# Two layer-norm tiles by ScalarE root, both sines later, first weights from ScalarE's queue, and a new order of loads and work

## The chip, the cores and the metric

The kernel runs on one core of a Trainium2 chip. The metric is the device time of one execution in microseconds. A core has TensorE (PE, matrix products into PSUM), VectorE (DVE), ScalarE (ACT, activations from tables that are loaded one set at a time), GpSimd (POOL), and SyncE (SP, which here only issues DMAs). ScalarE can issue DMAs too; its queue and SyncE's are separate queues on the same 16 DMA engines.

## The reference

```python
def _layernorm(x, axis=-1, eps=1e-5):
    m = jnp.mean(x, axis=axis, keepdims=True); v = jnp.var(x, axis=axis, keepdims=True)
    return (x - m) / jnp.sqrt(v + eps)

xn = _layernorm(A_q)                                   # 2048 x 512, bf16
# s: long convolution along the 2048 positions, one filter per channel
k_shift = sum over t of 4 taps: k shifted by t, times shift_k
kv = k_shift * A_v
y  = irfft(rfft(pad(kv)) * rfft(pad(ssm_k)))[:2048] + kv * ssm_D
s  = xn * y
# g: gated feed-forward, 512 -> 1792 -> 512
h  = gelu_tanh(xn @ w_gate) * (xn @ w_up)
g  = silu(h @ w_down)
out = A_q + s * g
```

## The kernel before

There are two halves on one core. The **feed-forward half** works on 16 tiles of 128 positions in four quarters q of four tiles. For each quarter: `ln` (statistics on VectorE, variance plus epsilon, the power -0.5 on GpSimd, then the normalised tile `XN`), a transpose of `XN` into `xnT`, 14 `unit`s m (a gate product with `Wg` and an up product with `Wu` of four matmuls each, GELU of the gate on ScalarE into `GE`, product on VectorE into `HT`), then `down`. In quarter 0 the transposes are done by TensorE against `ident`, and the units 0 and 1 are cut into pieces, so that they can begin with the first tiles: their products are single tiles of 128 columns (line 646, 128x128), and gelu and product are halves of 256 columns (lines 1197 and 1199). In quarters 1 to 3 the transpose is one DMA on SP (line 902), which needs the four normalised tiles of its quarter.

The **convolution half** turns the filter `Hn` (four blocks `h0` to `h3`, four `STREAM_TRANSPOSE`s on VectorE, line 931) and the shifted keys times values (lines 1017 to 1025, VectorE) into spectra by matmuls against tables of sines: `F1`/`FT` (first stage, lines 969 and 958) and `TF`, `MI` (second stage, line 1040). The tables are computed in the kernel: integer phases on VectorE (`f_mul`, `f_phase`, `m_parts`, `m_product`, `m_phase`), sines on ScalarE (`f_sin` writes `F1`, `m_sin` writes `TAB`), products `m_prod` twice and a sum `m_sum` on VectorE (lines 752 and 755) give `TF`, and `m_turn` (line 767, ScalarE, four instructions) gives `TFA` and `TFB`, which two DMA transposes on SP turn into `MI`.

**The order.** Each piece of work is a task, numbered in the order in which the code adds it. `SEQ` is a list of task numbers written out by hand; a number with `b` takes the task's second engine. Each engine runs its own tasks in the order in which they stand in `SEQ`, and waits in that order: an instruction whose input is not there holds up all behind it on its engine. Which PSUM bank or buffer slot a task gets is decided at build time from planned durations (`LAND` holds the planned landing times of loads). `ORDER` is the order of loads, all issued by SP.

In the kernel before, the orders around the start are:

- SP: x00 x01 x02 (tiles 0, 1, and 2 with 3 of quarter 0), wg0 wu0 (weights of units 0 and 1, 256 KB each), wg1 wu1, D, h0 h1 h2 h3, wg2 wu2, x1, taps, k0, ... v0 v1 k3 v2 v3, then the transpose of quarter 1.
- ACT: sine table load, `f_sin`, variance of tile 0, `m_sin` with the load of the GELU table, variance of tile 2, copies of the transposed tiles, gelus of units 0 and 1 and the copy of tile 3, gelu 2, gelu 4, last half of gelu 0, gelu 5, `swap_rows`, `m_turn`, gelu 6, ...
- DVE: phases, statistics and normalised tiles 0 to 3 with the two `m_prod`s and `m_sum` among them, halves of the products of units 0 and 1, h0 and h1 transposed, product 2, h2 transposed, product 4, h3 transposed, product 5, last half of product 0, product 6, statistics of tiles 4 to 7, ...
- PE: 12 warm-up matmuls, transposes of tiles 0 and 1, pieces of units 0 and 1 with the transposes of tiles 2 and 3, units 2, 4, 5, 3, 6, 9, 7 in part, and then the first filter stage (line 969).
- POOL: constants, four powers (tiles 0 to 3), four tap copies (line 998), the power of quarter 1, the addition `h_fold` (line 938), the powers of quarters 3 and 2.

Of the kernel before, what the change touches and what calls it, by code (L numbers as in the profile page):

```python
# [417 lines left out]
def build_kernel(nc, A_q, A_k, A_v, A_shift_k, A_ssm_k, A_ssm_D, B_w_gate, B_w_up, B_w_down, out):  # L418
    with ExitStack() as es0:
# [334 lines left out]
        def m_sum():
            D(lambda h: h.tensor_tensor(TF[:], TM[0][:], TM[1][:], ALU.add), R_TM, [R_MF])

        def sin(T, V, R_V, R_T, n=128):
            trk.op("ACT", lambda h: h.activation(T, V, ACTF.Sin, bias=COLS[0:n, 0:1], scale=SIN_SCALE), r=[*R_V, R_cols], w=[R_T])

        def m_sin(e):  # L760
            sin(TAB[:], PH[:], [R_PH], R_TAB)
            trk.op("ACT", lambda h: h.activation(COLS[:, 1:2], COLS[:, 0:1], ACTF.Gelu_apprx_tanh), r=[R_cols], w=[R_col1])
# [10 lines left out]
        def f_sin(e):  # L773
            sin(F1, C32[:].rearrange("p a c -> p (a c)"), [R_C32], R_F1)
        S.add([("ACT", 510.0)], f_sin, r=[bFP, bcq, bwarm], w=[bF1])
        S.add([("DVE", 800.0), ("ACT", 1600.0)], swap_rows, r=[bF1], w=[bFS])
# [87 lines left out]
        def ln(q):  # L864
# [4 lines left out]
            for h in range(1 if q else 4):  # L869
# [5 lines left out]
                def var(e, hd, ts=ts):  # L875
                    if e == "ACT":
                        return hd.activation(mv[:, ts, 2:3], mv[:, ts, 1:2], ACTF.Identity, bias=EPSC[:, 0, :], scale=1.0)
                    return hd.tensor_scalar(mv[:, ts, 2:3], mv[:, ts, 1:2], LN_EPS, None, ALU.add)  # L878
# [498 lines left out]
```

## Time and profile before

| | |
|---|---|
| median of 3 runs | 187.17 us (186.51 to 187.7) |
| span of the profiled execution | 185.7 us |
| own time of the profiled execution | not given beside its span; the median lies 1.5 us above the span |
| PE busy | 178.5 us (96%) |
| DVE busy | 165.4 us (89%) |
| ACT busy | 141.4 us (76%) |
| POOL busy | 11.9 us (6%) |
| bytes moved by DMA | 48.38 MB |

A row of the timeline gives start and duration in us, engine, line, operation, output<-input with shapes, and in brackets the idle time of the engine before it and what ended that. Rows that are merged have a count (x4), and their duration runs from the first start to the last end. Matmuls overlap one another, so that four of them of 512 columns show 1.03 us but follow each other every 0.87 us; instructions of VectorE overlap by some 0.08 us too.

### The profile page before, as it was taken

What the parts mean: (1) busy time and instruction counts of PE and PEld (TensorE: products, weight loads), DVE (VectorE), ACT (ScalarE), POOL (GpSimd) and SP (SyncE); (2) the same over time, 40 slices, a digit from 0 to 9 for tenths busy, and PEclk for the clock granted to TensorE, in tenths of its full rate; (3) what the DMA queues carried; (4) which work ended last, traced back from release to release, by engine and by line L of the source; (5) the groups of instructions that cost most, each with busy time, mean ns of one, the idle gap of its engine ahead of it and who ended that gap; (6) DMA issues with size and microseconds to landing.
All of it is one profiled execution on the core that took longest, in us unless ns stands there. A gap on an engine that the chain in (4) does not pass through costs nothing.

```text
span 185.7 us, 3808 instructions
## 1 busy us (share of the span) xinstructions
PE 178.5 (96%) x1513; PEld 77.9 (42%) x1522; DVE 165.4 (89%) x247; ACT 141.4 (76%) x205; POOL 11.9 (6%) x26
## 2 busy tenths in 40 slices
PE   8799799999999999999999999999999999999992
PEld 3564344444443443434443433433334344445451
DVE  6989999999999999999267998998999997694795
ACT  3745989956689999987965798898988686326971
POOL 4500044100000000020200000000000000000000
PEclk9999999999999999999999999999999999999999
DMA  5999999999964578979979998589746233699355
GB/s 132 337 406 376 280 346 369 397 416 257 257 232 165 186 243 266 325 241 369 222 271 205 335 333 276 177 272 317 254 163 217 76 116 119 205 359 389 141 180 196
DMA packets 38683, 48.38 MB, mean 260 GB/s; under 512 B 9483, under 2 KB 28427, under 8 KB 38666
## 3 DMA queue, kind: packets, MB, share of 16 engines
q1 hardware_dynamic: 32138, 39.76, 65.6%
q10 hardware_dynamic: 6528, 8.39, 13.8%
q8 instruction: 12, 0.20, 0.5%
q14 instruction: 5, 0.04, 0.1%
HBM read 27.39 MB, written 14.68 MB: 227 GB/s over the span
## 4 chain that ended last, share of the span: by engine, by line
PE 77%; DVE 9%; DMA 5%; ACT 5%; issue 2%; SPq 0%; ACTq 0%
PE psall L646 63%; PE psall L1040 5%; DMA Hn<-in_A_ssm_k_dram 4%; PE psall L1236 3%; PE psall L958 2%; PE psall L969 2%; DMA X<-in_A_q_dram 1%; ACT GE L1206 1%; DVE KTM L1021 1%; PE psall L1290 1%; ACT FT L637 1%; DVE HTr L931 1%; DVE G L1307 1%; DVE G L1258 1%; DVE G L1319 1%
## 5 line engine op out<-in xcount | busy, mean ns | idle before, releaser
L646 PE MATMUL psall<-xnT,Wu 128*128 128x512 bf16 (+1 forms) x248 | 55.9, 359 | 0.0
L646 PE MATMUL psall<-xnT,Wg 128*128 128x512 bf16 (+1 forms) x248 | 55.6, 359 | 0.0
L1206 ACT ACTIVATE GE<-psall 128x512 bf16<-128x512 f32 x54 | 32.2, 621 | 11.1 <-PE psall L646 7.0
L646 PE MATMUL psall<-Wd,HT 128*128 128x512 bf16 (+1 forms) x173 | 38.1, 367 | 0.7 <-ACT GE L1206 0.2
L646 PEld LDWEIGHTS psall<-xnT,Wu 128*128 128x128 bf16 x248 | 22.0, 98 | 26.5 <-issue 3.2
L646 PEld LDWEIGHTS psall<-xnT,Wg 128*128 128x128 bf16 x248 | 21.9, 98 | 26.1 <-issue 2.0
L1215 DVE TENSOR_TENSOR HT<-psall,GE 128x512 bf16<-128x512 f32 x36 | 24.2, 682 | 3.8 <-PE psall L646 3.6
L637 ACT ACTIVATE BO<-psall 128x1024 bf16<-128x1024 f32 x21 | 21.1, 1024 | 6.2 <-PE psall L1290 4.7
L646 PEld LDWEIGHTS psall<-Wd,HT 128*128 128x128 bf16 x182 | 16.3, 98 | 20.7 <-issue 3.4
L1143 DVE TENSOR_TENSOR HSW<-KB,HSW 128x2048 bf16<-128x2048 bf16 x16 | 19.2, 1215 | 0.0
L637 ACT ACTIVATE KB<-psall 128x1024 bf16<-128x1024 f32 x15 | 15.2, 1030 | 3.6 <-PE psall L1040 3.6
L637 ACT ACTIVATE HSW<-psall 128x1024 bf16<-128x1024 f32 x15 | 15.0, 1036 | 1.6 <-PE psall L1040 1.6
L1023 DVE TENSOR_TENSOR KAC<-KAC,KTM 128x2048 bf16<-128x2048 bf16 x12 | 14.6, 1214 | 0.0
L1021 DVE TENSOR_TENSOR KTM<-KK,SKB 128x2048 bf16<-128x2048 bf16 x12 | 14.6, 1213 | 0.0
L637 ACT ACTIVATE XN<-psall 128x1024 bf16<-128x1024 f32 x10 | 10.3, 1028 | 4.6 <-PE psall L969 3.3
L1236 PE MATMUL psall<-Wd,HT 128*64 128x512 bf16 (+1 forms) x112 | 12.5, 366 | 0.0
L1247 ACT ACTIVATE G<-psall 128x512 bf16<-128x512 f32 x12 | 6.9, 596 | 7.0 <-PE psall L646 7.0
L637 ACT ACTIVATE U__73<-psall 128x512 bf16<-128x512 f32 x18 | 11.5, 654 | 0.1
L867 DVE BATCH_NORM_STATS2 stats<-X 128x6 f32<-128x512 bf16 x16 | 10.5, 676 | 0.5 <-DMA X<-in_A_q_dram 0.5
L880 POOL TENSOR_TENSOR mv<-mv,NHALF 128x1 f32<-128x1 f32 (+1 forms) x7 | 6.5, 926 | 62.3 <-DVE mv L878 60.0
L1143 DVE TENSOR_TENSOR KB<-KB,HSW 128x2048 bf16<-128x2048 bf16 x8 | 9.6, 1216 | 0.0
L1166 DVE TENSOR_TENSOR HSW<-HSW 128x2048 bf16<-128x2048 bf16 x8 | 9.6, 1216 | 0.0
(89 smaller groups left out, 177.5 us busy)
## 6 DMA issues: line engine op xcount, KB each, us to landing
BH<-ZH SPq DMA_DIRECT2D x8, 512.0 KB, 4.6
HSW<-HSW SPq DMA_DIRECT2D x16, 256.0 KB, 3.6
BK<-ZK SPq DMA_DIRECT2D x8, 512.0 KB, 5.3
ZI<-BO ACTq DMA_DIRECT2D x16, 256.0 KB, 2.2
BI<-ZI SPq DMA_DIRECT2D x8, 512.0 KB, 6.5
ZH<-XN ACTq DMA_DIRECT2D x5, 512.0 KB, 5.6
ZK<-AST SPq DMA_DIRECT2D x5, 512.0 KB, 3.1
Hn<-in_A_ssm_k_dram SPq DMA_DIRECT2D x4, 512.0 KB, 8.3
```

What stands on the lines that cost most here:

```text
L637: return h.activation(o, i, ACTF.Copy, scale=scale)
L646: return h.matmul(o, lhsT=l, rhs=r, start=st, stop=sp)
L867: t_stats[t] = op([("DVE", 670.0)], lambda e, h, t=t: h.bn_stats(stats[:, t, :], X[:, t, :]), r=[bX[q][t % 4]], w=[bst[t]], rr=[R_X[t]], w ...
L1021: op([("DVE", dur)], lambda e, h, j=j, m=m: h.tensor_tensor(KTM[:, m.slot, :, :], kk(j), sk(j), ALU.mult), r=need + [bSKB[j], a], w=[m], r ...
L1023: op([("DVE", dur)], lambda e, h, m=m: h.tensor_tensor(KAC[:, a.slot, :, :], KAC[:, a.slot, :, :], KTM[:, m.slot, :, :], ALU.add), r=[m], ...
L1040: trk.op("PE", lambda h: h.matmul(ps(s, i)[b, :], lhsT=wt(col)[a, :], rhs=data(col)[a, :], start=n < 16, stop=n >= len(todo) - 16, tile_po ...
L1143: return hd.tensor_tensor(pair(KB, *(2 * DM * z for z in slots())) if to else x, k, x, ALU.mult)
L1166: return hd.tensor_tensor(x, x, y, ALU.add)
L1206: op([("ACT", act(512))], lambda e, h: h.activation(GE[:, g.slot, :], bank(pg), ACTF.Gelu_apprx_tanh), r=[pg], w=[g], rr=lambda: R_bank(pg ...
L1215: op([("DVE", dve(512, 1))], lambda e, h: h.tensor_tensor(HT[:, q % 2, m, :], bank(pu), GE[:, g.slot, :], ALU.mult), r=[pu, g], w=[bHT[q][m]],
L1236: trk.op("PE", lambda h, m=m, i=i, c=c: h.matmul(pc()[c, :], lhsT=HT[:, q % 2, m, 128 * jt + 64 * i:128 * jt + 64 * i + 64], rhs=Wd[:, m, ...
L1247: op([("ACT", act(n))], lambda e, h, g=g, pc=pc: h.activation(g, pc(), ACTF.Tanh, scale=0.5), r=[p], w=[bt], rr=lambda p=p: R_bank(p), ww= ...
```

## The change

- **Tiles 0 and 1** (`N_ROOT = 2`): ScalarE takes the root of variance plus epsilon, VectorE the reciprocal. The addition of epsilon and GpSimd's power stay for the other tiles.
- **Tables of ScalarE**: the first activation is a one-element root that loads the root's table; a one-element GELU loads the GELU table once the roots and the first copies are done; `f_sin` and `m_sin` become one task `sines`, which comes after the copy of tile 3, in front of the second halves of the gelus of units 0 and 1, and loads the GELU table again at its end.
- **Engines**: the tasks `m_prod`, `m_sum` and `m_turn` may run on POOL, and the new `SEQ` puts all of them there, behind `h_fold`.
- **Loads**: wg0 and wu0 are issued by ScalarE, right behind the one-element root. SP's order becomes x00 x01 x02 wg1 wu1 h0 h1 wg2 wu2 h2 h3 D x1 taps ..., with the transpose of quarter 1 ahead of v2 and v3.
- **Order** (the new `SEQ`, by engine):
  - ACT: root table, wg0, wu0, roots of tiles 0 and 1, copies of the transposed tiles 0 and 1 with the variance of tile 2 among them, GELU table, first halves of gelus 0 and 1, copy of tile 3, `sines`, second halves of gelus 0 and 1, gelus 2, 3, 5, 4, `swap_rows`, gelu 6, ...
  - DVE: phases (all but `m_phase`), statistics of tiles 0 and 1 with their reciprocals and normalised tiles, then those of tiles 2 and 3, copy of tile 2, `m_phase`, first halves of products 1 and 0, h0 and h1 transposed, second halves of products 1 and 0, products 2 and 3, h2 and h3 transposed, product 5, statistics, ...
  - PE: as before with other unit numbers; the same count of products stands ahead of the first filter stage.
  - POOL: constants, powers of tiles 2 and 3, tap copies, power of quarter 1, `h_fold`, `m_prod` twice, `m_sum`, `m_turn`, powers of quarters 3 and 2.
  - Later: the same tasks in a partly different order. Of the copies out of PSUM that either engine can do, VectorE has seven of those of 1024 columns after the key stages in the new order where it had four; two of them (outputs 6 and 4 of the last stage) stand at the start of the last stretch. Of the normalised tiles 8 to 11 VectorE does all four where it did one.

```diff
-ORDER = "x00 x01 x02 w0 w1 D0 h0 h1 h2 h3 w2 x1 s0 k0 w3 k1 d0 k2 d1 v0 v1 k3 v2 v3 x2 x3"
+ORDER = "x00 x01 w0 x02 w1 h0 h1 w2 h2 h3 D0 x1 s0 k0 w3 k1 d0 k2 d1 v0 v1 k3 v2 v3 x2 x3"
...
+N_ROOT = 2
...
-        def m_prod(i):
+        def m_prod(i, e):
...
-            D(lambda h: h.tensor_tensor(TM[i][:], a, b, ALU.mult), [R_TAB], [R_TM[i]])
+            D(lambda h: h.tensor_tensor(TM[i][:], a, b, ALU.mult), [R_TAB], [R_TM[i]], e)
...
-        def m_sin(e):
+        def gelu_table(e):
+            trk.op("ACT", lambda h: h.activation(COLS[:, 1:2], COLS[:, 0:1], ACTF.Gelu_apprx_tanh), r=[R_cols], w=[R_col1])
+
+        def sines(e):
+            sin(F1, C32[:].rearrange("p a c -> p (a c)"), [R_C32], R_F1)
             sin(TAB[:], PH[:], [R_PH], R_TAB)
-            trk.op("ACT", lambda h: h.activation(COLS[:, 1:2], COLS[:, 0:1], ACTF.Gelu_apprx_tanh), r=[R_cols], w=[R_col1])
+            gelu_table(e)
...
+        S.add([("ACT", 1480.0)], lambda e: trk.op("ACT", lambda h: h.activation(COLS[:, 2:3], ONE[:, 0:1], ACTF.Sqrt), w=[R_col2]), w=[bsq])
...
-            S.add([("DVE", 690.0)], lambda e, i=i: m_prod(i), r=[bTAB], w=[bTM[i]])
-        t_table = S.add([("DVE", 690.0)], lambda e: m_sum(), r=bTM, w=[bMF])
+            S.add([("DVE", 690.0), ("POOL", 1400.0)], lambda e, i=i: m_prod(i, e), r=[bTAB], w=[bTM[i]])
+        t_table = S.add([("DVE", 690.0), ("POOL", 1400.0)], m_sum, r=bTM, w=[bMF])
...
-            {"k": load_k, "v": load_v, "w": load_w, ...
+            {"k": load_k, "v": load_v, "w": lambda i: load_w(i, ("ACT", "ACT") if i == 0 else ("SP", "SP")), ...
...
+                if q == 0 and h < N_ROOT:
+                    op([("ACT", 300.0)], lambda e, hd, ts=ts: hd.activation(mv[:, ts, 2:3], mv[:, ts, 1:2], ACTF.Sqrt, bias=EPSC[:, 0, :], scale=1.0), r=[bconst, *bm], w=[be, bsq], rr=rm + [R_ep], ww=rm)
+                    op([("DVE", 160.0)], lambda e, hd, ts=ts: hd.reciprocal(mv[:, ts, 3:4], mv[:, ts, 2:3]), r=[be], w=[b], rr=rm, ww=rm)
+                else:
...
-        S.add([("ACT", 1900.0)], m_turn, r=[bMF], w=[bMF2])
+        t_gelu = S.add([("ACT", 1480.0)], gelu_table, r=[bwarm, bsq], w=[B("gelu")])
+        S.behind(t_sines, [t_gelu])
+        S.add([("ACT", 2100.0), ("POOL", 2200.0)], m_turn, r=[bMF], w=[bMF2])
```

More of the change, by code (lines that the diff above doesn't have):

```diff
@@ L51 @@
 ISSUE = 470.0
-LAND = {"x0_0": 2900, "x0_1": 3400, "x0_2": 4980, "wg0": 5950, "wu0": 6780, "wg1": 8500, "wu1": 10000, "D": 9850, "kz": 10800, "h0": 11350, "h1": 12650, "h2": 13950, "h3": 16000, "wg2": 17550, "wu2": 19050, "x1": 20750, "sk": 22600, "kh1": 23800, "kh113": 24000, "k0": 25100, "wg3": 26600, "wu3": 28100, "k1": 29400, "wd0": 32100, "k2": 33050, "wd1": 35940, "v0": 36790, "v1": 38070, "k3": 39360, "v2": 40580, "v3": 41890}
+LAND = {"x0_0": 3350, "x0_1": 3900, "wg0": 5000, "wu0": 5700, "x0_2": 6200, "wg1": 7900, "wu1": 9400, "h0": 10700, "h1": 12000, "wg2": 13500, "wu2": 15000, "h2": 16300, "h3": 17600, "D": 18000, "kz": 10800, "x1": 19500, "sk": 21500, "kh1": 23000, "kh113": 23200, "k0": 24600, "wg3": 26100, "wu3": 27600, "k1": 29000, "wd0": 31800, "k2": 33200, "wd1": 35700, "v0": 37200, "v1": 38600, "k3": 40000, "v2": 41400, "v3": 42700}
 W_XT, W_SW, W_BK, W_BH, W_ZI, W_BI, W_ZK, W_MI, W_G1 = 850000, 690000, 685000, 688000, 310000, 575000, 600000, 329000, 150000
@@ L302 @@
     SHARE_BW = 300.0
-    FIRST = {"loads": 300.0, "SP": 37000.0}
+    FIRST = {"loads": 300.0, "SP": 37000.0, "ACT": 1600.0}
     DRAIN, DRAIN2 = 121.0, 97.0
@@ L354, in run @@
         for name in SEQ.split():
-            t = self.tasks[int(name.rstrip("b"))]
-            eng, dur = t.opts[name[-1] == "b"]
+            t = self.tasks[int(name.rstrip("bc"))]
+            eng, dur = t.opts[{"b": 1, "c": 2}.get(name[-1], 0)]
             base = 0.0
@@ L542, in build_kernel @@
         R_id = res("ident", ident[:])
-        R_cols, R_col1 = (res(f"COLS{i}", COLS[:, i:i + 1]) for i in range(2))
+        R_cols, R_col1, R_col2 = (res(f"COLS{i}", COLS[:, i:i + 1]) for i in range(3))
         R_st = [res(f"st{t}", stats[:, t, :]) for t in range(NT)]
@@ L715, in warm_up @@
                 trk.op("PE", lambda h: mm(h, bank(warm), ONE[:, 0:128], ONE, True, True), w=R_bank(warm), accum=True)
-        t_warm = S.add([("PE", N_WARM * 427.0)], warm_up, w=[warm])
+        t_warm = S.add([("PE", 4650.0)], warm_up, w=[warm])
         bcq, bck, bFS = B("cq"), B("ck"), B("FS")
@@ L725, in build_kernel, with D @@
         SIN_SCALE = 2.0 * math.pi / TURN * (1.0 - 2e-6)
-        def D(fn, r, w):
-            trk.op("DVE", fn, r=r, w=w)
+        def D(fn, r, w, e="DVE"):
+            trk.op(e, fn, r=r, w=w)
         def f_mul():
@@ L748, in m_phase, with m_sum @@
             D(lambda h: h.tensor_scalar(PH[:], PH[:], TURN - 1, None, ALU.bitwise_and), [R_PH], [R_PH])
-        def m_prod(i):
+        def m_prod(i, e):
             a, b = TAB[:, NG * i:NG * i + NG].unsqueeze(2).broadcast_to([128, NG, 32]), TAB[:, 32 * i + 32:32 * i + 64].unsqueeze(1).broadcast_to([128, NG, 32])
-            D(lambda h: h.tensor_tensor(TM[i][:], a, b, ALU.mult), [R_TAB], [R_TM[i]])
-        def m_sum():
-            D(lambda h: h.tensor_tensor(TF[:], TM[0][:], TM[1][:], ALU.add), R_TM, [R_MF])
+            D(lambda h: h.tensor_tensor(TM[i][:], a, b, ALU.mult), [R_TAB], [R_TM[i]], e)
+        def m_sum(e):
+            D(lambda h: h.tensor_tensor(TF[:], TM[0][:], TM[1][:], ALU.add), R_TM, [R_MF], e)
         def sin(T, V, R_V, R_T, n=128):
             trk.op("ACT", lambda h: h.activation(T, V, ACTF.Sin, bias=COLS[0:n, 0:1], scale=SIN_SCALE), r=[*R_V, R_cols], w=[R_T])
-        def m_sin(e):
+        def gelu_table(e):
+            trk.op("ACT", lambda h: h.activation(COLS[:, 1:2], COLS[:, 0:1], ACTF.Gelu_apprx_tanh), r=[R_cols], w=[R_col1])
+        def sines(e):
+            sin(F1, C32[:].rearrange("p a c -> p (a c)"), [R_C32], R_F1)
             sin(TAB[:], PH[:], [R_PH], R_TAB)
-            trk.op("ACT", lambda h: h.activation(COLS[:, 1:2], COLS[:, 0:1], ACTF.Gelu_apprx_tanh), r=[R_cols], w=[R_col1])
+            gelu_table(e)
         def m_turn(e):
@@ L766, in m_turn @@
             for o, i, f, R in ((ta[:, :, 0], 0, 1.0, R_MFA), (ta[:, :, 1], 0, -1.0, R_MFA), (tb[:, :, 0], 1, 1.0, R_MFB), (tb[:, :, 1], 1, 1.0, R_MFB)):
-                trk.op("ACT", lambda h, o=o, i=i, f=f: h.activation(o, tf[:, :, i], ACTF.Copy, scale=f), r=[R_MF], w=[R])
+                trk.op(e, lambda h, o=o, i=i, f=f: copy(e, h, o, tf[:, :, i], f), r=[R_MF], w=[R])
         bFP, bQ, bMQ, bMF2 = B("fp"), B("q"), B("mq"), B("mf2")
@@ L772, in build_kernel @@
         S.add([("DVE", 340.0)], lambda e: f_phase(), r=[bFM], w=[bFP])
[L773 to L776, printed above, removed]
+        bsq = B("root")
+        S.add([("ACT", 1480.0)], lambda e: trk.op("ACT", lambda h: h.activation(COLS[:, 2:3], ONE[:, 0:1], ACTF.Sqrt), w=[R_col2]), w=[bsq])
         S.add([("DVE", 800.0)], lambda e: m_parts(), r=[bcq], w=[bQ])
@@ L781, in build_kernel @@
         S.add([("DVE", 480.0)], lambda e: m_phase(), r=[bMP], w=[bMQ])
-        t_sin = S.add([("ACT", 1900.0)], m_sin, r=[bMQ, bcq, bF1], w=[bTAB])
+        t_sines = S.add([("ACT", 3450.0)], sines, r=[bFP, bMQ, bcq, bwarm], w=[bF1, bTAB])
+        S.add([("DVE", 800.0), ("ACT", 2250.0)], swap_rows, r=[bF1], w=[bFS])
         bTM = [B(f"tm{i}") for i in range(2)]
         for i in range(2):
-            S.add([("DVE", 690.0)], lambda e, i=i: m_prod(i), r=[bTAB], w=[bTM[i]])
-        t_table = S.add([("DVE", 690.0)], lambda e: m_sum(), r=bTM, w=[bMF])
-        sin_tasks = [t_sin]
+            S.add([("DVE", 690.0), ("POOL", 1400.0)], lambda e, i=i: m_prod(i, e), r=[bTAB], w=[bTM[i]])
+        t_table = S.add([("DVE", 690.0), ("POOL", 1400.0)], m_sum, r=bTM, w=[bMF])
         x_dr = A_q[0].rearrange("(p t) d -> p t d", t=NT)
@@ L858, in build_kernel @@
                 continue
-            {"k": load_k, "v": load_v, "w": load_w, "x": load_x, "d": load_wd, "h": lambda i: load_h(i, "SP"), "s": load_taps, "D": load_d}[what[0]](int(what[1:]))
+            {"k": load_k, "v": load_v, "w": lambda i: load_w(i, ("ACT", "ACT") if i == 0 else ("SP", "SP")), "x": load_x, "d": load_wd, "h": lambda i: load_h(i, "SP"), "s": load_taps, "D": load_d}[what[0]](int(what[1:]))
         t_stats = [None] * NT
@@ L878, in var @@
                     return hd.tensor_scalar(mv[:, ts, 2:3], mv[:, ts, 1:2], LN_EPS, None, ALU.add)
-                t_var = op([("DVE", 180.0)] + ([] if q else [("ACT", 300.0)]), var, r=[bconst, bF1, *bm], w=[be], rr=rm + [R_ep], ww=rm)
-                t_pw = op([("POOL", 2500.0 if q else 600.0)], lambda e, hd, ts=ts, n=n: hd.tensor_tensor(mv[:, ts, 3:4], mv[:, ts, 2:3], NHALF[:, 0:n, :], ALU.pow),
-                          r=[bconst, be] + bm, w=[b], rr=rm + [R_nh], ww=rm)
+                if q == 0 and h < N_ROOT:
+                    op([("ACT", 300.0)], lambda e, hd, ts=ts: hd.activation(mv[:, ts, 2:3], mv[:, ts, 1:2], ACTF.Sqrt, bias=EPSC[:, 0, :], scale=1.0), r=[bconst, *bm], w=[be, bsq], rr=rm + [R_ep], ww=rm)
+                    op([("DVE", 160.0)], lambda e, hd, ts=ts: hd.reciprocal(mv[:, ts, 3:4], mv[:, ts, 2:3]), r=[be], w=[b], rr=rm, ww=rm)
+                else:
+                    t_var = op([("DVE", 180.0)] + ([] if q else [("ACT", 300.0)]), var, r=[bconst, *bm], w=[be], rr=rm + [R_ep], ww=rm)
+                    t_pw = op([("POOL", 2500.0 if q else 600.0)], lambda e, hd, ts=ts, n=n: hd.tensor_tensor(mv[:, ts, 3:4], mv[:, ts, 2:3], NHALF[:, 0:n, :], ALU.pow),
+                              r=[bconst, be] + bm, w=[b], rr=rm + [R_nh], ww=rm)
+                    t_pws.extend([t_var, t_pw])
                 bn = B(f"nb{q}_{h}")
@@ L891, in ln @@
                        r=[bX[q][t % 4], b] + ([bn] if q else []), w=[bXN[t]], rr=[R_X[t], R_mv[t], R_nb[t]], ww=[R_XN[t]], lat=0.0)
-                t_pws.extend([t_var, t_pw])
             return t_pws
@@ L1197, in unit @@
                     op([("ACT", act(256))], lambda e, h, p=p2[0], g=g2, c=c: h.activation(GE[:, g.slot, c], bank(p)[:, c], ACTF.Gelu_apprx_tanh), r=[p2[0]], w=[g2],
-                       rr=lambda p=p2[0]: R_bank(p), ww=lambda g=g2: [R_GE[g.slot]], after=sin_tasks)
+                       rr=lambda p=p2[0]: R_bank(p), ww=lambda g=g2: [R_GE[g.slot]], after=[t_gelu])
                     op([("DVE", dve(256, 1))], lambda e, h, p=p2[1], g=g2, c=c: h.tensor_tensor(HT[:, 0, m, c], bank(p)[:, c], GE[:, g.slot, c], ALU.mult), r=[p2[1], g2], w=[bHT[q][m]],
@@ L1204, in unit @@
             gu_tasks[q] += [tg, tu]
-            af = sin_tasks if q == 0 else []
             op([("ACT", act(512))], lambda e, h: h.activation(GE[:, g.slot, :], bank(pg), ACTF.Gelu_apprx_tanh), r=[pg], w=[g],
-               rr=lambda: R_bank(pg), ww=lambda: [R_GE[g.slot]], after=af)
+               rr=lambda: R_bank(pg), ww=lambda: [R_GE[g.slot]], after=[t_gelu] if q == 0 else [])
             af = (down_tasks[q - 2] if q >= 2 else []) + (s1_tasks["H"] if q == 1 else [])
```

44 rows, old and new, of the table SEQ are left out of this document.

## The prediction

> **What bounds the kernel now.** I read the busy shares first, then windows by stage, then the chain of waits, and the timelines around it. By windows (from:to in us, the window's length, busy time and count of PE, its weight loads, DVE, ACT, POOL; then clock, DMA share, GB/s):
>
> ```profile
> 30.00:37.00 7.00, 6.84 (x46) 3.08 (x45) 7.00 (x13) 6.79 (x12) 2.86 (x2) 1.00 1.07 389
> 37.00:60.00 23.00, 22.95 (x159) 9.71 (x158) 22.51 (x27) 17.27 (x25) 0.00 (x0) 1.00 0.89 264
> 60.00:88.00 28.00, 27.90 (x149) 11.24 (x150) 27.84 (x49) 25.97 (x38) 1.02 (x1) 1.00 0.80 273
> 88.00:110.00 22.00, 21.84 (x185) 9.07 (x186) 15.78 (x24) 17.05 (x24) 1.01 (x1) 1.00 0.97 272
> ```
>
> PE, with the largest busy time, is full from 30 us on. But from 30 to 88 us VectorE is just as full: it idles 0.65 us in 58. Only behind 88 us has it room (6.2 of 22). So both engines set the end up to 88 us, and PE alone after it. Where they meet shows in three rows: SP's transpose of quarter 3, the landing times of the three such transposes, and the products that need this one:
>
> ```profile
> 86.71 4.11 SPq L902 DMA_TRANSPOSE xnT<-XN x1
> DMA to landing us min/median/max: 6.9/7.3/8.3
> 94.19 3.61 PE L646 MATMUL psall<-xnT,Wg 128*128 128x512 bf16 x16
> ```
>
> 86.71 + 7.3 = 94.0, and PE uses it at 94.19. The transpose waits for tiles that VectorE (with ScalarE's help) normalises at the end of its full stretch, so a VectorE that is late there makes PE late nearly one for one. The rows of PE at the start:
>
> ```profile
> 0.76 4.85 PE L646 MATMUL psall<-const-bfloat16-1.0 128*128 128x512 bf16 x12 [0.76 <-PEq L1362]
> 6.28 0.40 PE L913 MATMUL psall<-ident,XN 128*128 128x128 bf16 x4 [0.67 <-DVE XN L889]
> 7.27 0.40 PE L913 MATMUL psall<-ident,XN 128*128 128x128 bf16 x4 [0.59 <-DVE XN L889]
> 7.50 0.39 PE L646 MATMUL psall<-xnT,Wu 128*128 128x128 bf16 x4
> 20.37 1.03 PE L646 MATMUL psall<-xnT,Wg 128*128 128x512 bf16 x4
> 21.99 0.28 PE L969 MATMUL psall<-HTr,FT 32*128 32x256 bf16 x2 [0.59 <-DVE HT L1215]
> 22.62 0.61 PE L969 MATMUL psall<-HTr,FT 32*128 32x256 bf16 x14 [0.35 <-ACT U__73 L637]
> ```
>
> PE waits 1.26 us for the first two normalised tiles, works without a gap from 7.50 to 21.40 (13.9 us), and waits 0.94 at the first filter stage, which needs all four transposes of the filter from VectorE, and PSUM that VectorE's products and ScalarE's copies free.
>
> **The change, part by part.** *Roots of tiles 0 and 1.* The path of tile 0 now:
>
> ```profile
> 3.31 0.69 DVE L867 BATCH_NORM_STATS2 stats<-X 128x6 f32<-128x512 bf16 x1 [0.51 <-DMA X<-in_A_q_dram]
> 4.52 0.29 ACT L877 ACTIVATE mv<-mv,EPSC 128x1 f32<-128x1 f32 x1 [1.50 <-DVE mv L868]
> 5.77 0.13 DVE L878 TENSOR_SCALAR mv<-mv 128x1 f32<-128x1 f32 x1
> 5.82 0.40 DVE L889 TENSOR_SCALAR XN<-X,mv 128x512 bf16<-128x512 bf16 x1
> ```
>
> The root is an activation of the same shape as the variance, 0.29; the reciprocal has no row: 0.13 (the one-element operation above) to 0.40, and I take 0.15, near the same shape. With phase work and tile 2's statistics out of the way, the statistics end at 4.0, their sum at 4.15, the root at 4.45 beside the second statistics, which end at 4.7; reciprocal, sum and normalisation bring tile 0 to 5.35 instead of 6.22, and tile 1 to about 6.0. The warm-up ends at 5.61, so the transposes run at 5.6 and 6.05, and with two copies the first product could start at 6.7 instead of 7.50: 0.8 us, if the weights are there.
>
> *First weights from ScalarE.* Issue on SP, a table load, and times from issue to landing by groups:
>
> ```profile
> 2.58 0.51 SPq L619 DMA_DIRECT2D Wu<-in_B_w_up_dram  x1
> 5.09 1.28 ACT L762 ACT_TABLE_LOAD   x1
> ...
> ZH<-XN ACTq DMA_DIRECT2D x5, 512.0 KB, 5.6
> ZK<-AST SPq DMA_DIRECT2D x5, 512.0 KB, 3.1
> ...
> Wu<-in_B_w_up_dram SPq DMA_DIRECT2D x1, 256.0 KB, 4.5
> ```
>
> wu0 lands at 2.58 + 4.5 = 7.1 now. On ScalarE the two issues stand behind a table load (1.28, from 0.73) and a one-element activation (0.2), so at about 2.25 and 2.7: nothing is gained there. SP issues its next 1 MB, wg1 and wu1, 1 us earlier than before, and they now run beside wg0 and wu0 instead of behind them. How queues share is seen at ScalarE's stores of 512 KB, which run beside the queued loads: 5.6, against 3.1 for SP's stores of as much when the loads are done. Bounds for wu0: 6.5 (served alone, without tile 2 and 3 ahead of it) and 7.1 + 2.5 = 9.6 (the whole difference is lost); 2.7 + 5.6 = 8.3 is nearest to a row and taken. The Trainium skill, DMA: Bandwidth & Descriptors, Queues, rings and completion order, says that each DMA engine goes round-robin between the queues that have work, a packet at a time. By that rule alone wu0 would land toward the late end of these bounds.
>
> *The first filter stage hides both.* PE needs its 13.9 us from the first product to that stage: 22.2 with weights at 8.3, 20.6 with weights in time. VectorE's path there:
>
> ```profile
> 5.05 7.20 DMA Hn<-in_A_ssm_k_dram
> ...
> 12.28 3.95 DVE L931 STREAM_TRANSPOSE HTr<-Hn 128x1024 int32<-128x1024 int32 x2 [0.93 <-DMA Hn<-in_A_ssm_k_dram]
> 19.23 2.03 DVE L931 STREAM_TRANSPOSE HTr<-Hn 128x1024 int32<-128x1024 int32 x1
> 21.19 0.65 DVE L1215 TENSOR_TENSOR HT<-psall,GE 128x512 bf16<-128x512 f32 x1
> 21.76 0.41 DVE L1199 TENSOR_TENSOR HT<-psall,GE 128x256 bf16<-128x256 f32 x1
> ```
>
> As many bytes (2.5 MB) stand ahead of h0 as before, so VectorE starts the transposes near 12.25 again. The last ends at 21.26 now; the new order puts two half products (0.34 each without the overlap) and the same number of full ones between: 21.95. Product 5 then frees PSUM at 22.55, against 21.84. So the stage starts between 22.0 and 22.6 whatever PE does before, as long as weights land by 8.7. VectorE's own order is level soon after: before, another half product and a wait for ScalarE's copy follow product 5, in the new order neither. These edits together: 0, with -0.3 if h0 lands earlier, and +0.9 if wu0 lands at 9.6. What goes as PE's wait at 6 and 7 us comes back as a longer one at 21.
>
> *ScalarE's tables.* `sines` is two loads of 1.28, two sines of 0.40 and less, and a dummy, 3.5 us, behind which the second halves of gelus 0 and 1 and gelu 2 wait, and behind those VectorE's products after the second filter transpose, at 16.2. It starts near 11.8, behind the copy of tile 3, and ends at 15.3; two half gelus end at 16.0. Hidden, with 0.2 us to spare; without that cover each us would be one at the filter stage. The early GELU load lies under the wait for weights. `m_turn` leaves ScalarE just ahead of the filter stage.
>
> *GpSimd gets the second-stage tables.* VectorE is freed of three instructions ahead of the 0.93 us that it waits for h0: worth nothing. GpSimd gets seven instructions behind `h_fold`, from 33 us on, where VectorE has no idle time. Does GpSimd disturb VectorE? `h_fold` with the VectorE instruction beside it and all of that line, the tap copies, and VectorE's products out of PSUM (line 1215) in the stretch concerned:
>
> ```profile
> 32.49 0.92 POOL L938 TENSOR_TENSOR HTr<-HTr,Dt 128x128 bf16<-128x128 bf16 x1
> 33.04 0.39 DVE L884 SCALAR_TENSOR_TENSOR NB__68<-mv 128x4 f32<-128x4 f32 x1
> L884 DVE SCALAR_TENSOR_TENSOR NB__68<-mv x3: 131/166/385, 33.0 to 89.5; 128x4 f32<-128x4 f32 x3
> 22.81 2.47 POOL L998 COPY SKB<-SKR 128x512 bf16<-128x512 bf16 x4 [14.55 <-DMA SKR<-in_A_shift_k_dram]
> 33.00:43.00 10.00, 1.35 (x2) 1.00 1.07 404
> ```
>
> `h_fold` ran to 33.41. VectorE's 4-element operation, issued at 33.04, ended at 33.43, after 0.39 instead of 0.13: it reads as if it had waited for `h_fold`, 0.25 us for 128 columns. For 512 columns that is 1.0 for each of `m_prod` twice and `m_sum`, 3.0; a copy of 512 columns takes 0.62, so 0.31 for each of four `m_turn`s of 256, 1.2. Bounds: 0 (GpSimd always waits) and 4.2. In 33 to 43 us only 1.35 of VectorE's 10 us are products out of PSUM; nearly all else has two SBUF inputs, like the operation held. I take 0.85 of the 3.0, and nothing for the copies, since no row shows a copy holding VectorE: 2.55. Of it VectorE's one later wait gives back 0.46:
>
> ```profile
> 58.11 0.69 DVE L977 TENSOR_TENSOR X<-X 128x1024 bf16<-128x1024 bf16 x1 [0.46 <-ACT X L637]
> ```
>
> So +2.1 at the transpose of quarter 3, and at the end. The Trainium skill, SBUF — State Buffer, Who interferes with whom, says that VectorE and GpSimd share a port pair under an exclusive lock, which also catches VectorE operations with two SBUF inputs while GpSimd reads. The rows of `h_fold` agree; by that rule the copies count too, 1.0 more.
>
> *The rest.* v2 and v3 behind the transpose of quarter 1, and D later: their readers stand far behind in their engines' orders. In the last stretch two copies go to VectorE, which waits there now:
>
> ```profile
> 170.09 0.69 DVE L1307 TENSOR_TENSOR G<-BO,G 128x1024 bf16<-128x1024 bf16 x1 [2.36 <-ACT BO L637]
> ```
>
> A ScalarE copy of that shape takes 1.0, so two fit into 2.36. Other swaps in the order: no row prices them; I allow 0.5 either way.
>
> **Sum.** The profiled execution is this long, and the median of the runs lies 1.5 above it:
>
> ```profile
> span 185.7 us, 3808 instructions
> ```
>
> 185.7 + 2.1 = 187.8 for the span; 187.2 + 2.1 = 189.3 for the time.
>
> **Rivals.** (1) *GpSimd yields*, on the other side: no change. VectorE's operations overlap by 0.08 us, and if the shared access passes from one to the next, GpSimd waits; its tables are read only by the second stages, much later. For it: a single instruction of 0.39 is all that speaks for a hold. Against it: `h_fold` did get in between two VectorE operations. It decides at the first boundary after 33 us; time 187.2, from 186.6 to 187.9. (2) *Weights late*: wu0 at 9.6, PE reaches the filter stage at 23.5, and VectorE's transposes start 0.6 late, since half products stand ahead of them: +0.9 without GpSimd's hold, 188.1; with it 190.2. (3) *The early start is kept*: weights in time, and h0 earlier by more than the 0.3 I allow, since SP issues it nearly 2 us earlier. Then PE keeps 0.8 and saves the 0.94 at the filter stage: 185.5. Against it: the DMA engines move the same bytes ahead of h0.
>
> **How the numbers follow.** Forecast, GpSimd holds VectorE: 0.5, at 189.3, from 188.2 (half the price) to 191.2 (full price with late weights). Rival 1: 0.3. Rival 2 alone: 0.1. Rival 3: 0.1. The range keeps nearly all of the forecast and rivals 1 and 2: 186.5 to 191.0. A measurement of this kernel can tell 1% (1.9 us) from no change. Above 189.04 lie some seven tenths of the forecast and a little of rival 2, taken with the unpriced swaps: 0.38. Below 185.3 lies part of rival 3: 0.07. The rest, 0.55, is within 1%.
>
> **What would show it.** Forecast right: VectorE's tap products (lines 1021 and 1023) in 33 to 45 us with some near 2 us instead of 1.2, GpSimd's products near 1 us, SP's transpose of quarter 3 issued near 89 instead of 86.71. Rival 1: tap products at 1.2, GpSimd's products much longer. Early part: PE's first transpose at 5.6, the filter stage between 22.0 and 22.7. First product of 128 columns at 8.3; at 9.5 it is rival 2, at 6.7 rival 3 is open. I am wrong in another way if PE shows waits of over 1 us in all behind 100 us, where I priced the new order at nothing.

## The result, and the profile after

The changed kernel takes 189.47 us (median of 4 runs, 189.18 to 190.47), beside 187.05 us for the kernel before in the same comparison. The ratio is 1.0143 (95% interval 1.0106 to 1.0179), so the change costs 2.0 to 3.3 us. The profiled execution took 189.26 us with a span of 187.4 us; before, the span was 185.7 us. Each traced run that gives both has its time 1.8 to 1.9 us above its span, so the traced execution of the kernel before took about 187.6 us, more than its median: the spans differ by 1.7 us, the medians by 2.4. Line numbers of the changed kernel are 3 to 10 higher: 649 for 646, 980 for 969, 1225 for 1215, 1259 for 1249.

The windows of the changed kernel, by the same stages as in the prediction (from:to, length, PE, its weight loads, DVE, ACT, POOL, clock, DMA share, GB/s):

```profile
30.00:37.00 7.00, 7.00 (x60) 2.93 (x57) 6.69 (x10) 5.38 (x9) 6.64 (x4) 1.00 1.06 390
37.00:60.00 23.00, 19.70 (x129) 8.66 (x129) 22.90 (x26) 15.61 (x21) 5.38 (x6) 1.00 0.85 258
60.00:88.00 28.00, 28.00 (x156) 11.24 (x154) 27.80 (x42) 25.69 (x38) 1.04 (x1) 1.00 0.68 227
88.00:110.00 22.00, 22.00 (x172) 9.08 (x171) 18.95 (x35) 15.03 (x22) 1.01 (x1) 1.00 1.03 277
```

PE loses 3.3 us between 37 and 60 us, where it lost nothing before, and it is full from there on. VectorE stays full in that stretch. So the loss sits in one place, some 40 us ahead of the transpose of quarter 3 at which the prediction expected it to show. Rows picked from PE's timeline of the changed kernel (start, duration, instruction, and in brackets the idle time before and what ended it) show the start and the two later waits:

```profile
6.18 0.40 PE L922 MATMUL psall<-ident,XN 128*128 128x128 bf16 x4 [1.31 <-DVE XN L899]
6.86 0.40 PE L922 MATMUL psall<-ident,XN 128*128 128x128 bf16 x4 [0.28 <-DVE XN L899]
7.21 0.62 PE L649 MATMUL psall<-xnT,Wu 128*128 128x128 bf16 x8
21.73 0.62 PE L980 MATMUL psall<-HTr,FT 32*128 32x256 bf16 x16 [0.19 <-DVE HTr L940]
38.06 5.14 PE L649 MATMUL psall<-Wd,HT 128*128 128x512 bf16 x23 [0.88 <-DVE HT L1225]
49.74 0.61 PE L980 MATMUL psall<-HTr,FT 32*128 32x256 bf16 x14 [2.42 <-DVE G L1259]
```

The first filter stage is done at 22.35 instead of 23.23, so this execution is 0.9 us ahead there. Then PE waits 0.88 + 2.42 = 3.30 us, both times for VectorE. The trace of the kernel before shows gaps of 0.16 us and less behind 30 us, but it holds 1513 matmuls where this one and that of experiment 2 hold 1522, so these gaps are most likely missing records, and they are left out. 3.30 - 0.9 = 2.4; the end behind the last matmul is 0.3 us shorter; that leaves 2.1, and the spans differ by 1.7. The other 0.4 is not accounted for.

Why VectorE is late shows when GpSimd's timeline is laid beside VectorE's, both of the changed kernel:

```profile
33.56 3.56 POOL L755 TENSOR_TENSOR TM<-TAB 128x512 f32<-128x512 f32 x2
37.20 1.33 POOL L758 TENSOR_TENSOR TF<-TM,TM 128x512 bf16<-128x512 f32 x1
38.59 1.36 POOL L643 COPY TFA<-TF 128x256 bf16<-128x256 bf16 x1
40.04 0.94 POOL L642 TENSOR_SCALAR TFA<-TF 128x256 bf16<-128x256 bf16 x1
40.89 1.78 POOL L643 COPY TFB<-TF 128x256 bf16<-128x256 bf16 x2
```

```profile
34.68 1.53 DVE L988 TENSOR_TENSOR X<-X 128x1024 bf16<-128x1024 bf16 x1
36.14 1.26 DVE L1222 TENSOR_TENSOR HT<-U__73,GE 128x512 bf16<-128x512 bf16 x1
37.33 0.68 DVE L1225 TENSOR_TENSOR HT<-psall,GE 128x512 bf16<-128x512 f32 x1
37.93 1.69 DVE L1032 TENSOR_TENSOR KTM<-KK,SKB 128x2048 bf16<-128x2048 bf16 x1
39.54 0.63 DVE L1222 TENSOR_TENSOR HT<-U__73,GE 128x512 bf16<-128x512 bf16 x1
40.09 1.42 DVE L1034 TENSOR_TENSOR KAC<-KAC,KTM 128x2048 bf16<-128x2048 bf16 x1
41.44 0.90 DVE L988 TENSOR_TENSOR X<-X 128x1024 bf16<-128x1024 bf16 x1
42.26 1.43 DVE L1032 TENSOR_TENSOR KTM<-KK,SKB 128x2048 bf16<-128x2048 bf16 x1
```

With GpSimd still, these shapes take 0.68 (128x1024), 0.42 (128x512, two inputs in SBUF) and 1.21 (128x2048). The excess is 0.85 and 0.84 beside the products, 0.48 beside the sum, and 0.21 beside each of the four copies: 3.0 us in all. The one instruction with an input in PSUM (37.33) keeps its 0.68, though GpSimd's sum runs beside it.

### The profile page after: what moved, and what is told of

Its sections match the earlier page's. It is cut to its first block, busy times and chain, and to the rows that moved or that the text cites. A ratio compares the mean times of both kernels' runs of the same rounds, so it can differ in the third digit from the quotient of the medians.

```text
span 187.4 us, 3808 instructions
## 1 busy us (share of the span) xinstructions
PE 178.4 (95%) x1522; PEld 77.8 (42%) x1522; DVE 172.5 (92%) x251; ACT 138.4 (74%) x200; POOL 19.6 (10%) x31
## 4 chain that ended last, share of the span: by engine, by line
PE 66%; DVE 21%; DMA 6%; SPq 3%; POOL 2%; issue 1%; DVEq 0%
PE psall L649 55%; DMA Hn<-in_A_ssm_k_dram 6%; PE psall L1051 6%; DVE KTM L1032 3%; SPq L622 3%; DVE KAC L1034 3%; PE psall L969 2%; DVE G L1329 2%; DVE G L1317 2%; DVE HTr L940 2%; PE psall L1246 2%; POOL mv L889 2%; DVE HT L1225 1%; DVE HT L1222 1%; DVE X L988 1%
## 5 line engine op out<-in xcount | busy, mean ns | idle before, releaser
L649 PE MATMUL psall<-xnT,Wg 128*128 128x512 bf16 (+1 forms) x248 | 56.6, 359 | 0.0
L649 PE MATMUL psall<-Wd,HT 128*128 128x512 bf16 (+1 forms) x182 | 40.3, 368 | 0.9 <-DVE HT L1225 0.9
L1216 ACT ACTIVATE GE<-psall 128x512 bf16<-128x512 f32 x54 | 31.6, 608 | 11.7 <-PE psall L649 10.0
L640 ACT ACTIVATE BO<-psall 128x1024 bf16<-128x1024 f32 x19 | 19.0, 1028 | 6.0 <-PE psall L1051 3.2
L640 ACT ACTIVATE KB<-psall 128x1024 bf16<-128x1024 f32 x14 | 14.0, 1035 | 3.7 <-PE psall L1051 3.7
L1032 DVE TENSOR_TENSOR KTM<-KK,SKB 128x2048 bf16<-128x2048 bf16 x12 | 15.3, 1272 | 0.0
L889 POOL TENSOR_TENSOR mv<-mv,NHALF 128x4 f32<-128x4 f32 (+1 forms) x5 | 6.1, 1212 | 58.8 <-DVE mv L883 53.4
L640 ACT ACTIVATE X<-psall 128x1024 bf16<-128x1024 f32 x8 | 8.2, 1028 | 4.0 <-PE psall L980 3.9
L640 ACT ACTIVATE U__73<-psall 128x512 bf16<-128x512 f32 x18 | 10.9, 617 | 0.3 <-PE psall L649 0.3
L640 ACT ACTIVATE AST<-psall 128x1024 bf16<-128x1024 f32 x10 | 10.1, 1029 | 1.1 <-PE psall L969 0.9
```

The lines of the kernel that those rows point to most:

```text
L640: return h.activation(o, i, ACTF.Copy, scale=scale)
L649: return h.matmul(o, lhsT=l, rhs=r, start=st, stop=sp)
L1032: op([("DVE", dur)], lambda e, h, j=j, m=m: h.tensor_tensor(KTM[:, m.slot, :, :], kk(j), sk(j), ALU.mult), r=need + [bSKB[j], a], w=[m], r ...
```

## The experiments

All ratios below are against runs of the kernel before on the same chip, interleaved with them. There the kernel before took 186.4 to 186.5 us, 0.6 less than the 187.05 from which the expectations in microseconds were made; the ratios carry the verdicts. The two theories at the start: **the hold** (GpSimd's instructions hold VectorE, VectorE holds PE) and its rival, **the order** (the new sequence puts the instructions that PE waits for too far back on VectorE). The early part of the change is a question of its own.

**1. Tables early.** The changed kernel with GpSimd's seven table instructions right behind the sines, where VectorE transposes (one input) and multiplies out of PSUM. Only GpSimd's order changes.

```diff
 SEQ:
-... 11 86 32 12 367 355 ...   418 456 14b 15b 133 ...   137 16b 113 ...   525 76b 126 ...
+... 11 86 32 12 14b 15b 16b 76b 367 355 ...   418 456 133 ...   137 113 ...   525 126 ...
```

> The kernel after, with GpSimd's table work (two products, sum, four copies) moved from behind h_fold to right behind the sines, where VectorE transposes the filter and multiplies out of PSUM. Theory 'GpSimd's hold': VectorE's instructions between 33 and 43 us lose their 3.0 us of excess, PE's waits of 0.88 at 38 us and 2.4 at 49.7 us go, and the gain of the early start (0.7 to 0.9 us) stays: 186.2 to 186.6. Rival 'the new order makes PE wait': the wait of 2.4 us stays and the time is 189.5. If GpSimd holds the filter transposes as well, the filter stage starts up to 3 us later than 21.7 and the time is 187 to 189.

Measured: 186.36 us, ratio 0.9997 (0.9965 to 1.0030). GpSimd in this run, and the three VectorE instructions in the place of those held:

```profile
13.59 2.06 POOL L755 TENSOR_TENSOR TM<-TAB 128x512 f32<-128x512 f32 x2 [3.59 <-ACT TAB L761]
15.72 1.27 POOL L758 TENSOR_TENSOR TF<-TM,TM 128x512 bf16<-128x512 f32 x1
```

```profile
34.98 0.68 DVE L988 TENSOR_TENSOR X<-X 128x1024 bf16<-128x1024 bf16 x1
35.59 0.41 DVE L1222 TENSOR_TENSOR HT<-U__73,GE 128x512 bf16<-128x512 bf16 x1
36.52 1.21 DVE L1032 TENSOR_TENSOR KTM<-KK,SKB 128x2048 bf16<-128x2048 bf16 x1
```

PE's waits between 37 and 60 us in this run, 1.05 us in the place of 3.30:

```profile
46.98 0.62 PE L980 MATMUL psall<-HTr,FT 32*128 32x256 bf16 x14 [0.22 <-DVE G L1259]
...
51.78 0.61 PE L980 MATMUL psall<-HTr,FT 32*128 32x256 bf16 x14 [0.83 <-ACT X L640]
```

This trace is of an execution of 187.76 us, 1.4 above the median, so its other times may not be typical.

The excess is gone, and GpSimd itself takes 1.03 us for a product instead of 1.78: where the two met, each had waited for the other. VectorE's filter transposes beside it are not held (3.99 us for two, 3.94 in the changed kernel). The whole loss of 1.4% goes with it. But the early gain that the theory added is not there: the time is that of the kernel before.

**2. Tables late in the kernel before.** The reverse: products, sum and copies on GpSimd behind `h_fold`, nothing else.

```diff
...
+            S.add([("DVE", 690.0), ("POOL", 1400.0)], lambda e, i=i: m_prod(i, e), r=[bTAB], w=[bTM[i]])
+        t_table = S.add([("DVE", 690.0), ("POOL", 1400.0)], m_sum, r=bTM, w=[bMF])
...
+        S.add([("ACT", 1900.0), ("POOL", 2200.0)], m_turn, r=[bMF], w=[bMF2])
 SEQ: 14b 15b 16b 75b behind 54 (h_fold)
```

> The kernel before, with the two products, the sum and the four copies given to GpSimd behind h_fold, and nothing else changed. Theory 'GpSimd's hold': VectorE's two-input operations between 33 and 43 us grow by 2.5 to 3 us in all and the time by as much less the 0.46 us that VectorE waits later: 189.0 to 190.0. Rival 'the new order makes PE wait': 187.1, no change, since VectorE and ScalarE have less to do.

Measured: 188.54 us, ratio 1.0112 (1.0072 to 1.0152). The excess on VectorE is 2.5 us, for instance

```profile
33.80 0.99 DVE L1214 TENSOR_TENSOR HT<-U__73,GE 128x512 bf16<-128x512 bf16 x1 [0.20 <-ACT GE L1208]
34.71 2.06 DVE L1025 TENSOR_TENSOR KAC<-KAC,KTM 128x2048 bf16<-128x2048 bf16 x1
```

0.57 and 0.85 over the usual. The old order loses 2.1 us (1.3 to 2.8) by this one move, where 1.9 to 2.9 over the kernel before was expected, though VectorE and ScalarE have less to do. The hold does not need the new order.

**3. Only the copies late.**

```diff
 SEQ:
-... 32 12 367 355 ...   456 14b 15b 133 ...   137 16b 113 ...
+... 32 12 14b 15b 16b 367 355 ...   456 133 ...   137 113 ...
```

> The kernel after, with the products and the sum early on GpSimd as in the first kernel, and only the four copies of 256 columns behind h_fold. If copies hold VectorE too: 0.85 us of excess on VectorE's instructions near 33 to 37 us, and 0.4 to 0.9 us more than the first kernel. If only operations with two inputs hold: the same time as the first kernel.

Measured: 187.12 us, ratio 1.0031 (1.0000 to 1.0063). That is 0.6 us over the first experiment; the two intervals overlap, so the time alone does not decide, but VectorE's timeline does:

```profile
34.81 0.90 DVE L988 TENSOR_TENSOR X<-X 128x1024 bf16<-128x1024 bf16 x1
35.63 0.61 DVE L1222 TENSOR_TENSOR HT<-U__73,GE 128x512 bf16<-128x512 bf16 x1
37.90 0.63 DVE L1222 TENSOR_TENSOR HT<-U__73,GE 128x512 bf16<-128x512 bf16 x1
```

Three instructions are held by 0.2 us each. Copies, with one input, hold VectorE too.

**4. The products done twice** (the second time with the same values).

```diff
+            for _ in range(2):
                 D(lambda h: h.tensor_tensor(TM[i][:], a, b, ALU.mult), [R_TAB], [R_TM[i]], e)
```

> The kernel after, with each of the two products on GpSimd done twice (the second writes the same values again). Theory 'GpSimd's hold': 1.7 us more excess on VectorE's instructions from 33 us on, and 1.5 to 2.0 us more time: 191.0 to 191.5. Rival 'the new order makes PE wait': 189.5, no change, since GpSimd's results are read much later.

Measured: 193.14 us, ratio 1.0365 (1.0314 to 1.0415), 4 us over the changed kernel instead of the 1.5 to 2.0 expected. VectorE's excess is 4.5 us, 1.5 more, near the 1.7 expected. The rest is PE's; its timeline and the windows there, and for comparison one row of the first experiment's timeline and one window of the changed kernel:

```profile
51.10 1.03 PE L981 MATMUL psall<-HTr,FT 32*128 32x256 bf16 x14 [3.87 <-DVE G L1260]
52.07 5.54 PE L649 MATMUL psall<-Wd,HT 128*128 128x512 bf16 x14
```

```profile
50.00:52.00 2.00, 0.90 (x14) 0.42 (x14) 2.00 (x3) 0.00 (x0) 0.00 (x0) 0.51 0.17 33
52.00:54.00 2.00, 2.00 (x7) 0.72 (x6) 1.97 (x4) 1.94 (x3) 0.00 (x0) 0.50 0.04 8
54.00:56.00 2.00, 2.00 (x6) 0.70 (x5) 2.00 (x4) 0.49 (x1) 0.00 (x0) 0.50 0.70 262
56.00:58.00 2.00, 2.00 (x22) 0.74 (x20) 2.00 (x3) 0.36 (x1) 0.00 (x0) 0.79 0.00 0
```

```profile
47.53 3.20 PE L649 MATMUL psall<-Wd,HT 128*128 128x512 bf16 x14
```

```profile
50.00:52.00 2.00, 2.00 (x22) 0.87 (x11) 1.97 (x3) 1.57 (x3) 0.00 (x0) 1.00 0.07 15
```

PE waits 3.87 us instead of 2.42, 1.45 more, and then the granted clock is 0.5 until some 57 us: 14 matmuls of 512 columns take 5.54 us, where 14 take 3.20 in the first experiment. The two together are 1.45 + 2.3 for these, and 0.4 for the 14 filter matmuls (1.03 for 0.61): 4.2. The changed kernel's wait of 2.42 us leaves the clock at 1.00. The Trainium skill, TensorE: Matmul & The Clock Gate, HAM oscillation — how this bites in real kernels, says that PE is clocked down to half after gaps of over about 3.4 us. These two runs stand on both sides of that figure, and the wait of 3.34 us in experiment 5, after which the clock fell too, lies close to it.

**5. The first weights by SyncE again**, on the first experiment's kernel, twice: between x01 and x02, as the text of `ORDER` has them, and behind x02, as before.

```diff
-"w": lambda i: load_w(i, ("ACT", "ACT") if i == 0 else ("SP", "SP"))
+"w": lambda i: load_w(i, ("SP", "SP"))
 SEQ, second version only: x02 ahead of wg0 wu0
```

> The first experiment's kernel (GpSimd's tables early), with the first weights wg0 and wu0 issued by SyncE again, between x01 and x02. Theory 'second queue': the second queue is what brings the first filter block at 11 instead of 12.3 us; here SyncE issues everything behind them about 1 us later, the block lands near 12.3 again, the filter stage starts 0.5 to 1.0 us later than in the first experiment and the time is 0.5 us longer (ratio to before near 1.002). Rival 'the small load D is what delayed the block in the kernel before': it still lands near 11, and the time is that of the first experiment (0.9997) within 0.3%.

> The first experiment's kernel (GpSimd's tables early), with the first weights wg0 and wu0 issued by SyncE behind tile 2 and 3's load x02, as in the kernel before; the roots, the sines and all else stay. Prediction's step 'nothing is gained by ScalarE's issue': the tiles land earlier (x02 near 5 us), wu0 near 7 us, the first product at 7.1 to 7.5 us, and the time is that of the first experiment (ratio 0.9997 within 0.2%). Theory 'second queue': the filter blocks are issued 1 us later and land 0.5 to 1 us later, and the time is 0.3 to 0.8 us longer (ratio 1.002 to 1.004).

Measured: 187.57 us, 1.0050 (1.0016 to 1.0084), for the first, and 186.71 us, 0.9997 (0.9973 to 1.0022), for the second. In the first, tile 2 lands late (VectorE waits 3.27 us for it, to 8.84), ScalarE's variance of tile 2 stands ahead of the second copy of tile 1, and PE waits for that copy:

```profile
9.78 0.29 ACT L882 ACTIVATE mv<-mv,EPSC 128x1 f32<-128x1 f32 x1 [3.34 <-DVE mv L873]
```

```profile
10.40 0.40 PE L649 MATMUL psall<-xnT,Wu 128*128 128x128 bf16 x4 [3.34 <-ACT xnT L640]
24.98 0.62 PE L980 MATMUL psall<-HTr,FT 32*128 32x256 bf16 x16
```

Here too the clock falls, to 0.58 in the window from 11 to 13 us:

```profile
11.00:13.00 2.00, 2.00 (x26) 2.00 (x24) 1.63 (x6) 1.61 (x5) 0.37 (x1) 0.58 1.03 381
```

The filter stage comes 2.75 us later than in the first experiment (22.23), and the time grows by 1.0 us. In the second version the stage is at 22.39 and the time does not change. So neither queue is better here; what costs is x02 behind the first weights on one queue. Whether the second queue brings the filter block earlier stays open. VectorE's transposes start at 11.62 in the second version. In the seven traces with the second queue they start at 11.00 (the changed kernel), 11.09, 11.11, 11.20, 11.35, 11.58 and 12.13 (the first experiment), so mostly up to 0.6 us earlier, but once later; the time does not show it.

**6. D behind the filter blocks**, in the kernel before.

```diff
 SEQ:
-... 22 23 24 25 26 27 28 29 ...
+... 22 23 25 26 27 28 24 29 ...
```

> The kernel before, with the small load D moved from ahead of the four filter blocks to behind them, nothing else. Theory 'second queue': the first filter block lands at 12.3 us as before and the time stays (ratio 1.000). [...]

Measured: 186.67 us, 1.0016 (0.9986 to 1.0045). The transposes start at 11.70, where they start at 12.28 and, in experiment 2, at 12.26 with D ahead, so D may delay the block. One trace does not show it, since with one order of loads this start varied between 11.00 and 12.13; the time does not fall.

**7. Powers instead of roots**, on the first experiment's kernel.

```diff
-N_ROOT = 2
+N_ROOT = 0
```

> The first experiment's kernel (GpSimd's tables early), with the addition of epsilon on VectorE and GpSimd's power for the tiles 0 and 1 again instead of ScalarE's root and VectorE's reciprocal. Prediction's step 'the roots are worth 0.8 us at the first product, and the filter stage hides it': the first product starts 0.3 to 0.8 us later than in the first experiment, the filter stage not later, and the time is the same (ratio 0.9997 within 0.2%). Rival 'PE keeps the early start': 0.3 to 0.8 us more (ratio 1.002 to 1.004).

Measured: 186.49 us, 0.9988 (0.9959 to 1.0017). PE's timeline:

```profile
7.94 0.62 PE L649 MATMUL psall<-xnT,Wu 128*128 128x128 bf16 x8
22.05 0.62 PE L980 MATMUL psall<-HTr,FT 32*128 32x256 bf16 x16
```

The first product is 0.4 us later than in the first experiment (7.53), the filter stage is not, and the time is the same. The roots are worth nothing here.

**8. The first gate operation earlier**, on the first experiment's kernel, and **9.** that with the powers of experiment 7.

```diff
 SEQ:
-... 138 115 141 429 121 45 430 142 ...
+... 138 115 429 121 45 430 141 142 ...
```

On VectorE this puts the tap sum (task 141, line 1034) behind the gate of tile 0 (line 1259) instead of ahead of it.

> The first experiment's kernel (GpSimd's tables early), with VectorE's first gate operation (line 1259), which PE waits for near 47 us, moved ahead of the tap sum that stands before it, so 1.1 us earlier. Theory 'what the early start gains is lost at VectorE's gate': PE's wait near 47 to 52 us goes and the time falls by 0.2 to 0.8 us (ratio to before 0.995 to 0.999). Rival 'VectorE's total work up to 88 us sets the end': same time as the first experiment (0.9997), the wait comes back elsewhere.

> The first experiment's kernel with GpSimd's powers instead of the roots and with the first gate operation ahead of the tap sum, the two edits that each left the time as it was or a little below. If PE's work behind the filter stage (158 us without waits) sets the end, nothing is left to gain: ratio to before 0.998 to 1.000. If the two add up: 0.995 to 0.997.

Measured: 186.49 us, 0.9995 (0.9975 to 1.0016), and 186.97 us, 1.0013 (0.9991 to 1.0036). PE's waits near 47 and 52 us go, and the time does not. So the two edits do not add up to the 0.995 to 0.997 that one theory gave: in experiment 9's trace PE waits 0.3 us in all between 24 us and its last matmul, so its waits leave next to nothing to gain. No version beats the kernel before by more than a measurement can tell.

## Why the prediction was right, and where its terms were off

189.3 us was forecast, 189.47 measured, inside the range, and the mechanism is the one forecast: GpSimd's work behind `h_fold` holds VectorE. That is shown in both directions (experiments 1 and 2) and on VectorE's rows by the dose (4), and rival 1, GpSimd yields, is refuted by VectorE's rows.

- **The price of the hold**: 2.55 was forecast, 3.0 measured. The products and the sum cost 2.2, not 2.55, and the copies 0.8, where the step took nothing since no row showed a copy holding VectorE. One instruction, `h_fold`, carried the whole estimate. The Trainium skill, SBUF — State Buffer, Who interferes with whom, which the prediction cites, has it that a GpSimd instruction contends when it reads SBUF, so that copies count too. Experiment 3 bears that out at 0.2 us for each copy, where the prediction worked out 1.0 for the four. Given back are 0.4 us (VectorE idles 0.10 us between 37 and 60 us, before 0.49), near the 0.46 forecast, so 2.6 net instead of 2.1; the ratios with the hold and without it (1.0143 and 0.9997) say 2.7. That the time came within 0.2 us of the forecast is in part luck: two errors went opposite ways, products and sum priced 0.4 too high, copies 0.8 too low.
- **The path to PE**: the step was not the one that came to bear. VectorE's delay was to reach PE through the transpose of quarter 3. That transpose is late, issued at 89.89 (forecast near 89, before 86.71), but PE comes to its products with no wait; these are its issue and the first product that needs it:

```profile
89.89 3.40 SPq L911 DMA_TRANSPOSE xnT<-XN  x1
```

```profile
96.44 1.02 PE L649 MATMUL psall<-xnT,Wg 128*128 128x512 bf16 x4
```

  PE had lost its time before that, waiting for VectorE's product at 38 us and for its gate at 49.7. PE is full from there on, so what it lost there is still lost at the end. The three transposes land a median of 6.1 us after their issue in this run, so this one near 96.0: late enough to hold PE nearly as long, had PE come earlier. That is why the amount came out near the forecast.
- **Where it shows on VectorE**: not near 2 us on the tap products (1.69 at most), but on whatever two-input instruction meets GpSimd (X and HT above). GpSimd's products are near 1 us, as forecast, only beside transposes and PSUM (experiment 1); here they take 1.78, which is what rival 1 said of GpSimd. Each holds the other, so the two were no alternatives.
- **First weights**: the step was wrong. ScalarE's issues do not stand behind the table load, they run beside it; ScalarE's timeline in the changed kernel, and its weights in the issue table:

```profile
0.73 1.28 ACT L781 ACT_TABLE_LOAD   x1 [0.73 <-PEq L1372]
0.79 0.44 ACTq L622 DMA_DIRECT2D Wg<-in_B_w_gate_dram  x1
1.26 0.53 ACTq L622 DMA_DIRECT2D Wu<-in_B_w_up_dram  x1
...
Wu<-in_B_w_up_dram ACTq DMA_DIRECT2D x1, 256.0 KB, 5.1
```

  wu0 lands at 1.26 + 5.1 = 6.4, below the lower bound of 6.5 and not at 8.3; 7.1 before. The time from issue to landing was well taken (5.6 forecast); the place of the issue was not. Rival 2, weights late, has no ground.
- **Roots**: tile 0 is normalised at 6.12, not 5.35. VectorE waits 0.96 us for tile 1's load, with tile 0's reciprocal queued behind tile 1's statistics. The loads of tiles 0 and 1 take 3.0 us from issue to landing (median) beside the weights on the other queue, and 2.2 with the weights behind them on one queue (experiment 5, second version); there the wait is gone and the transposes do start at 5.83.
- **The filter stage hides both**: as a statement on the time it held. Without the hold the whole change gives 0.9997; roots, queue and gate order each move that ratio by 0.001 or less (experiments 7, 5, 8), with intervals of about 0.003 either way. Its numbers did not: VectorE's transposes start at 11.00 and not 12.25, and the stage starts at 21.73, below the 22.0 forecast. In this one execution the stage was done 0.9 us ahead, at 22.35 against 23.23, near rival 3 in part. But in two other traces of the old order (experiments 2 and 6) it was done at 22.81 and 22.85, and in the other runs of the new order with weights on time at 22.4 to 23.0, so most of the 0.9 belongs to these two executions.
- **The rest at 0 ±0.5**: without the hold, held. Behind 100 us PE shows no wait in the changed kernel.
- **Two figures that do not follow**: the upper end of 191.2 is not the sum of its terms (187.2 + 0.9 + 3.0 - 0.46 = 190.6 without the copies, 191.8 with them), and the 2.5 MB ahead of h0 are 2.0 without h0 itself. Neither changes the forecast.

What stays open: why VectorE's filter transposes start 1.1 us apart (11.00 and 12.13) in two runs with one order of loads, and so what the early part is worth by itself: by the first experiment's interval no more than 0.35% either way.

## What to carry to other kernels

Before moving work to an idle GpSimd, read which VectorE instructions will run beside it: those with two inputs in SBUF pay the rest of GpSimd's instruction, those out of PSUM and the transposes here paid nothing, so the same work was free at 14 us and cost 2.7 us at 34. Price the hold by count: each GpSimd instruction that meets VectorE's full stretch costs up to its own duration, copies too. A time gained ahead of a wait for another engine is worth what that wait leaves of it; here 0.4 us at the first product was worth nothing.

## What the runs showed of the hardware that was not expected

ScalarE issued two DMAs at 0.79 and 1.26 us while its table load ran from 0.73 to 2.01. PE's granted clock fell to about half after waits of 3.34 and 3.87 us, and not after 2.42; in experiment 4 the half clock cost 2.7 us, more than the 1.45 us of longer wait. GpSimd and VectorE delay each other both ways: 1.03 us to 1.78 for a product, 0.42 us to 1.26 for VectorE's.
